# Two transformer layers on one core: 250 pairs of row maxima beside the projections in place of 223, and sixteen key tiles kept in place of twelve

## The chip, the cores and the metric

The kernel runs on one core of a Trainium2 chip. The metric is the device time of one execution in microseconds, as the median of several runs. The engines are named as in the profile: PE (TensorE matmuls), PEld (its weight loads), DVE (VectorE), ACT (ScalarE), POOL (GpSimd) and SP (SyncE, which issues most of the DMAs here).

## The reference

A block of attention A and a block of two dense layers B are applied twice, A, B, A, B, each on the normalised rows and added back to them. There are 2048 rows of 640 columns, 32 heads of 20 columns, and an inner width of 1536; both passes use the same weights.

```python
def _A_ref(x, wqkv, wo):
    qkv = (x @ wqkv).reshape(B, S, 3, H, Dh)      # transposed to 3, B, H, S, Dh
    q, k, v = qkv
    scores = einsum("bhqd,bhkd->bhqk", q, k) * (Dh ** -0.5)
    o = einsum("bhqk,bhkd->bhqd", softmax(scores), v)
    return o.transpose(0, 2, 1, 3).reshape(B, S, D) @ wo
def _B_ref(x, w1, b1, w2, b2):
    r = max(x @ w1 + b1, 0)
    return (r * r) @ w2 + b2

x = A_x
x = x + _A_ref(_layernorm(x), A_wqkv, A_wo)
x = x + _B_ref(_layernorm(x), B_w1, B_b1, B_w2, B_b2)
x = x + _A_ref(_layernorm(x), A_wqkv, A_wo)
x = x + _B_ref(_layernorm(x), B_w1, B_b1, B_w2, B_b2)
```

## The kernel before, in words

Each layer has three stages: `qkv` (the projections to queries, keys and values), `attention`, and the output projection with the dense layers (`add_heads`, `mlp`). The program is written out in a fixed order; each engine works through its instructions in that order, and waits where a semaphore says so. Matrix operands are split in a high and a low part (`split_to` on ACT and DVE, `split_on_pool` on ACT and POOL), so that a projection is three matmuls per block of 128 inner columns (`THREE`).

**Projections.** The rows are cut in four blocks `tb` of 512. `front` loads, normalises (DVE: statistics L252, L253, normalising L260) and transposes (PE, L362) one block into five tiles `xnT`. A unit (`proj_unit`, 15 matmuls, L304) makes 128 columns of queries or keys for one block; there are 40 units. `UNITS` has first the four units of each block that hold the first head groups (`FIRST` = 4), block after block, and then the other six for all four blocks. The result goes to memory (`d_qk`) through SP one unit later (`later`, `pending`). Sixteen value units (`v_unit`, 30 matmuls of 320 columns, L332) follow.

**Row maxima.** The softmax needs the maximum of each query row over all 2048 keys. A *pair* is one 128-query piece `sub` of a block of 512 queries, against one tile of 512 keys `c`, for the two heads `par` of a pair `p`: two matmuls (L433) and the maxima over their results on DVE. Heads come in groups `g` of four; a block of queries is `t = 4 g + qb`, and has 32 pairs; a layer has 32 blocks and 1024 pairs. A *group of work* `(g, qb, c)` has eight pairs.

Part of the pairs is done beside the projections: `between` is called after every projection matmul with a cost (1 for a projection matmul, 0.65 for a value matmul), and each time the sum reaches a threshold it calls `some`, which takes three pairs from the list `work`, refilled group by group from `groups`. There a pair writes two adjacent banks (`Twos`, three such pairs of banks) and one reduction reads both (`smax_two`, L454). `tiles` asks for a group's key tile and query tile (`load_k`, `load_q`: six DMAs on SP each, and two more for the rows of ones in a key tile that is made for the first time) when the group ahead of it is taken. `groups` is filled from `EARLY[tb]` at the end of the fourth unit of block `tb`, with the groups whose query and key blocks are there by then, and at the last block with all groups of head group 1.

The other pairs are done in `attention`, where each half of a pair has its own reduction (`smax`, L445).

**Attention.** Blocks follow each other; each has 16 key tiles of 128 keys. For a key tile there are four scores (L499: 62 rows of contraction, since two rows hold the maximum that is to be subtracted), four exponentials on ACT (L506) and the product with the values (L511, accumulated in bank 7). The scores of heads `par` 0 and 1 lie in different rows of the PE array, as do the two halves of a pair of maxima. The order is a string of letters: `a`, `b` a score of either half, `m`, `n` half a pair of maxima, `V` the product with the values. `ORDERS[n]` has eight key tiles (32 scores, eight `V`) and `n` pairs; `pairs` picks `n` between 12 and 16 for each round, so that no block of queries is reached by the scores before its maxima are done:

```python
most = max([8 * (e + 1 - n) / max(t * NKT - 5 - i, 1) for t, e in ends.items() if e >= n], default=0)
state["debt"] += most
n = min(max(round(state["debt"]), 12), 16)
state["debt"] -= n
```

After a block's last maximum `mrows_max` and `mrows` turn its maxima into the two extra rows of the query tile (one transposition on PE, L474, a copy on ACT, two operations on POOL, eight DMAs). After a block's last key tile `finish` copies the accumulators (ACT, L524) and POOL and SP do the division later on. `begin` does what is due when a key tile is begun: it loads queries, values, and in the first four key-tile groups of a head group the key tiles of the next head groups into `kept`, a ring of tiles indexed by `g % 3` and `c`.

All tiles of 4 KB per partition come from one pool of 42 slots.

Of the kernel before, what the change touches and what calls it, by code (L numbers as in the profile page):

```python
# [9 lines left out]
F32R = mybir.dt.float32r  # L10
# [6 lines left out]
P = 128  # L17
# [7 lines left out]
QB = 512  # L25
NQB = S // QB
NG = H // 4
# [11 lines left out]
def tile_layers(  # L39
# [26 lines left out]
    def slot(shape, dtype, label):  # L66
        return arena.tile(shape, dtype, tag="slot", name=name(label))
# [315 lines left out]
    k_t, q_t, v_t, mx_t, kept = {}, {}, {}, {}, {}  # L383
# [12 lines left out]
    def load_k(g, c, keep):  # L396

        if not keep:
            k = slot([P, 2, QB], F32R, "k")
        elif (g % 3, c) in kept:  # L400
            k = kept[g % 3, c]
        else:
            k = kept[g % 3, c] = slot([P, 2, QB], F32R, "k")
            for par in range(2):
                dma(nc.sync, k[64 * par + 60 : 64 * par + 62], d_one)
        k_t[g, c] = k
        rows_of_heads(k, 1, KSEG, g, c)
# [171 lines left out]
    def prep_job():  # L579
# [13 lines left out]
    EARLY = [  # L593
        [(0, qb, c) for qb in range(NQB) for c in range(NQB) if max(qb, c) == tb]
        for tb in range(NQB)
    ]
    EARLY[-1] += [(1, qb, c) for qb in range(NQB) for c in range(NQB)]

    FIRST = 4
# [3 lines left out]
    def qkv(first, x_src, rest):  # L605
# [4 lines left out]
        state = {"pace": 0, "n": 0}  # L610
# [13 lines left out]
            else:  # L624
                at(early, n, lambda pos=pos: w_qk.need(pos * 10, pos * 10 + 9))
        for k in range(KD if first else w_v.n):
            n = len(UNITS) - 7 + k
            if first:
                at(early, n - 2, lambda k=k: raws.append(raw_rows(wqkv[:, 2 * D :], k)))
                at(late, n, lambda k=k: w_v.put(  # L630
                    raws.pop(0), k * 4, k * 4 + 2, 2, nc.scalar.copy, pool_lo
                ))
            else:
                at(early, n, lambda k=k: w_v.load(k))
# [18 lines left out]
        def end_group(x):  # L653
            g, qb, c = x
            t = g * NQB + qb
            left[t] -= 1
            if left[t]:
                return
            if t < 1:
                mrows_max(t)  # L660
                work.append(lambda: mrows(ps_q, t))
            elif t > 2:
                del q_t[t]
# [20 lines left out]

        def between(cost):
            state["pace"] += cost
            if state["pace"] >= 11:
                state["pace"] -= 11
                some()
            state["n"] += 1  # L690
            if state["n"] % 4 == 0:
                next(rest, None)

        for n, (tb, pos) in enumerate(UNITS):
            while tb not in xt_:
                next(rest)
            run(early, n)
            later(proj_unit(pos, tb, lambda: between(1)))
            run(late, n)
            if pos == FIRST - 2:  # L700
                tiles(EARLY[tb][0])
            if pos == FIRST - 1:
                groups.extend(EARLY[tb])
            if first:
                w_qk.save_full(1)
                w_v.save_full(1)
            if pos >= FIRST and tb == NQB - 1 or n == 4 * FIRST - 1:
                w_qk.past(pos * 10 + 9, w_qk.got)
# [26 lines left out]
    def attention(first, x_src, first_rows):  # L735
# [25 lines left out]
        def begin(i):  # L761
# [6 lines left out]
                    load_q(t + 2)  # L768
            if u % 4 == 1 and qb == 0:
                k_t.pop((g - 1, u // 4), None)  # L770
                for h in (1, 2):
                    if g + h < NG and (g + h, u // 4) not in k_t:
                        load_k(g + h, u // 4, True)
                if g and g + 2 >= NG:
                    del kept[(g - 1) % 3, u // 4]
            if u in (2, 10) and qb == NQB - 1 and g + 1 < NG:
                load_v(g + 1, u // 8)
            if first and t < 16 and u % 6 == 3:
# [300 lines left out]
```

## Time and profile before

| | us |
|---|---|
| median of 3 runs | 3805.24 (3803.75 to 3805.78) |
| profiled run: time | 3801.84 |
| profiled run: span | 3799.8 |
| first layer: projections from the start to the first score | 334.2 |
| first layer: first score to the last product with the values | about 1153 |
| second layer: first score | 2224.3 |
| busy in the span: PE, DVE, ACT, POOL | 3754.3, 2923.8, 2399.9, 813.0 |
| granted clock of PE, mean | 0.997 |

The rows of the prediction come from one profiled execution. A row of a group of instructions reads: line, engine, operation, output<-input, shapes, count, then total busy microseconds and mean nanoseconds of one, then idle time of the engine just before them and who ended it. A row of the timeline reads: start, length in microseconds, engine, line, operation, count of instructions merged in it, and in brackets the idle time ahead of it and its releaser. A row of the chain of waits reads: start, length, what the end of the program was waiting for.

### The profile page before, as it was taken

The numbers are of one execution on the slowest core, as the hardware profiler recorded it, in microseconds if no ns is written. First come the engines' busy times: TensorE is split into PE (matmuls) and PEld (weight loads), VectorE is DVE, ScalarE is ACT, GpSimd is POOL, SyncE is SP. The second block draws the span as 40 slices with busy tenths as digits, with TensorE's granted clock in tenths as the row PEclk, the third lists the DMA queues.
The fourth block names the chain that finished last, engine by engine and source line by source line (L and its number), as shares of the span: only waits on it lengthen the run. The fifth ranks groups of instructions, "written<-read, shape, count | busy, mean of one in ns | idle before, by whom it ended". The sixth has DMA issues, their size and how long they took to land.

```text
span 3799.8 us, 62979 instructions
## 1 busy us (share of the span) xinstructions
PE 3754.3 (99%) x23636; PEld 2142.9 (56%) x23636; DVE 2923.8 (77%) x4436; ACT 2399.9 (63%) x4663; POOL 813.0 (21%) x889
## 2 busy tenths in 40 slices
PE   7999999999999999999999999999999999999999
PEld 5676444443443435988876754444444444369998
DVE  7999999999999992444469989999999999924443
ACT  2115999999999996122211159999999999951221
POOL 5430343221121111111143201211211111101110
PEclk9999999999999999999999999999999999999999
DMA  6553454322121135611244422222222211355111
GB/s 191 176 189 110 132 142 149 107 71 73 49 70 42 31 96 176 239 42 42 93 142 157 161 89 59 65 74 53 65 81 53 59 40 42 101 191 209 42 42 42
DMA packets 228073, 378.72 MB, mean 100 GB/s; under 512 B 47740, under 2 KB 96636, under 8 KB 227768
## 3 DMA queue, kind: packets, MB, share of 16 engines
q1 hardware_dynamic: 227224, 372.98, 31.1%
q8 instruction: 187, 3.06, 0.3%
q10 hardware_dynamic: 544, 1.71, 0.2%
q14 instruction: 118, 0.97, 0.1%
HBM read 243.00 MB, written 130.52 MB: 98 GB/s over the span
## 4 chain that ended last, share of the span: by engine, by line
PE 94%; DVE 3%; DMA 1%; ACT 1%; SPq 0%; issue 0%; POOL 0%; ACTq 0%; DVEq 0%; POOLq 0%
PE banks L511 26%; PE banks L293 20%; PE banks L499 18%; PE banks L433 18%; PE banks L304 6%; PE banks L332 4%; DVE mx L445 1%; DVE mx L454 1%; SPq L75 0%; PE banks L909 0%; PE banks L474 0%; ACT e L506 0%; DMA k<-d_qk 0%; DVE bst L252 0%; DVE h L265 0%
## 5 line engine op out<-in xcount | busy, mean ns | idle before, releaser
L506 ACT ACTIVATE e<-banks 128x512 f32<-128x512 f32 x4096 | 2113.8, 619 | 159.4 <-PE banks L499 104.7
L445 DVE TENSOR_REDUCE mx<-banks 128x1 f32<-128x512 f32 x3204 | 2002.5, 685 | 209.4 <-PE banks L433 147.5
L433 PE MATMUL banks<-k,q 60*128 60x512 f32 x4096 | 1197.5, 442 | 8.7 <-DMA q<-d_qk 4.1
L499 PE MATMUL banks<-q,k 62*128 62x512 f32 x4096 | 1174.9, 430 | 4.5 <-ACT e L506 1.7
L511 PE MATMUL banks<-e,vg 128*32 128x512 f32 x8192 | 1092.8, 605 | 0.0
L433 PEld LDWEIGHTS banks<-k,q 60*128 60x128 f32 x4096 | 580.7, 184 | 626.9 <-DVE mx L445 495.3
L499 PEld LDWEIGHTS banks<-q,k 62*128 62x128 f32 x4096 | 613.6, 185 | 438.6 <-ACT e L506 399.9
L454 DVE TENSOR_REDUCE mx<-banks 128x2 f32<-128x1024 f32 x446 | 518.8, 1220 | 49.6 <-PE banks L433 37.0
L555 POOL TENSOR_TENSOR few<-few,minus_t 128x16 f32<-128x16 f32 x62 | 179.8, 2901 | 991.1 <-DMA few<-d_s 975.3
L511 PEld LDWEIGHTS banks<-e,vg 128*32 128x32 f32 x8192 | 161.5, 108 | 346.0 <-issue 322.8
L293 PE MATMUL banks<-w,h 128*128 128x320 f32 x2304 | 352.8, 312 | 2.9 <-DVE h L265 2.7
L293 PEld LDWEIGHTS banks<-w,h 128*128 128x128 f32 x2304 | 340.9, 189 | 12.5 <-DVE h L265 6.8
L293 PE MATMUL banks<-xnT,w 128*128 128x512 f32 x1440 | 330.3, 390 | 0.0
L304 PE MATMUL banks<-xnT,wqk 128*128 128x512 f32 x1200 | 311.9, 407 | 0.0
L932 ACT ACTIVATE r<-banks,b_t 128x512 f32<-128x512 f32 x96 | 66.2, 690 | 375.2 <-PE banks L293 375.2
L293 PEld LDWEIGHTS banks<-xnT,w 128*128 128x128 f32 x1440 | 269.4, 188 | 55.3
L270 ACT COPY r<-banks 128x512 f32<-128x512 f32 x92 | 53.7, 588 | 334.9 <-PE banks L304 292.5
L304 PEld LDWEIGHTS banks<-xnT,wqk 128*128 128x128 f32 x1200 | 220.8, 192 | 68.9 <-issue 23.8
L952 DVE TENSOR_TENSOR x<-banks,x 128x320 f32<-128x320 f32 x128 | 62.8, 491 | 200.9 <-PE banks L293 194.9
L566 POOL TENSOR_TENSOR o<-o 128x512 f32<-128x512 f32 x62 | 79.5, 1282 | 560.0 <-PE banks L433 177.4
L933 DVE TENSOR_TENSOR r<-r 128x512 f32<-128x512 f32 x96 | 79.4, 827 | 132.6 <-ACT r L932 132.2
L887 DVE TENSOR_TENSOR x<-banks,x 128x320 f32<-128x320 f32 x64 | 31.0, 484 | 171.0 <-PE banks L293 77.7
(63 smaller groups left out, 1704.1 us busy)
## 6 DMA issues: line engine op xcount, KB each, us to landing
q<-d_qk SPq DMA_DIRECT2D x636, 80.0 KB
d_qk<-ev SPq DMA_DIRECT2D x80, 512.0 KB
k<-d_qk SPq DMA_DIRECT2D x384, 80.0 KB
x<-d_x SPq DMA_DIRECT2D x96, 320.0 KB
d_o<-ot SPq DMA_DIRECT2D x248, 80.0 KB
ot<-d_o SPq DMA_DIRECT2D x38, 512.0 KB
d_v<-v SPq DMA_DIRECT2D x32, 512.0 KB
vg<-d_v SPq DMA_DIRECT2D x32, 512.0 KB
```

Of the source, the lines that this page charges most:

```text
L293: nc.tensor.matmul(dst, a, b, start=(n == 0), stop=(n == last))
L304: nc.tensor.matmul(dst, w_qk.piece(pos * 10 + hw * KD + k), xt_[tb][k][:, hx, :], start=(n == 0), stop=(n == 3 * KD - 1),)
L332: nc.tensor.matmul(dst[:, :HALF], xt_[tb][k][:, hx, i * P : (i + 1) * P], w_v.piece(k * 4 + hw * 2 + hf), start=(j == 0), stop=(j == 3 * K ...
L433: nc.tensor.matmul(dst, q_t[t][b : b + 60, p, sub * P : (sub + 1) * P], k_t[t // NQB, c][b : b + 60, p, :], start=True, stop=True,)
L445: nc.vector.tensor_reduce(maxima(t)[:, 2 * p + par, sub, c : c + 1], dst, axis=AX.X, op=ALU.max)
L454: nc.vector.tensor_reduce(maxima(t)[:, 2 * p : 2 * p + 2, sub, c], dst, axis=AX.X, op=ALU.max)
L499: nc.tensor.matmul(dst, k_t[t // NQB, kt // 4][b : b + 62, p, (kt % 4) * P : (kt % 4 + 1) * P], q_t[t][b : b + 62, p, :], start=True, stop ...
L506: nc.scalar.activation(es[p][:, par, :], dst, AF.Exp, scale=SCALE)
L511: nc.tensor.matmul(acc[32 * h : 32 * h + 32, :], v_t[t // NQB, kt // 8][:, kt % 8, 32 * h : 32 * h + 32], es[p][:, par, :], start=(kt == 0 ...
L555: nc.gpsimd.tensor_tensor(few, few, minus_t, op=ALU.pow)
L566: nc.gpsimd.tensor_mul(o[:, 0, :], o[:, 0, :], o[:, 1, :])
L933: nc.vector.tensor_mul(r, r, r)
```

## The change

In the projections `between` calls `some` at every 10 units of pace, not 11. The groups of a block of rows are handed over after the first unit of the next block (`n % FIRST == 0`), not after the block's own fourth unit, and the first group's tiles are asked for one unit later; one group of head group 1 is handed over after unit 5, ahead of those of block 1. The last list holds the groups of head groups 1 and 2. The value weights are prepared from two units later on, in the second layer two slots per unit. In attention the ring of key tiles has four head groups, and `begin` loads three groups ahead.

The instructions that result: 249 pairs per layer are issued beside the projections where there were 223, and the number of matmuls is the same.

```diff
-        elif (g % 3, c) in kept:
-            k = kept[g % 3, c]
+        elif (g % 4, c) in kept:
+            k = kept[g % 4, c]
         else:
-            k = kept[g % 3, c] = slot([P, 2, QB], F32R, "k")
+            k = kept[g % 4, c] = slot([P, 2, QB], F32R, "k")
...
-    EARLY[-1] += [(1, qb, c) for qb in range(NQB) for c in range(NQB)]
+    EARLY[-1] += [(g, qb, c) for g in (1, 2) for qb in range(NQB) for c in range(NQB)][1:]
...
         for k in range(KD if first else w_v.n):
-            n = len(UNITS) - 7 + k
+            n = len(UNITS) - 5 + (k if first else k // 2)
...
             if left[t]:
+                if t >= NQB and groups and groups[0][:2] != (g, qb):
+                    del q_t[t]
                 return
...
             state["pace"] += cost
-            if state["pace"] >= 11:
-                state["pace"] -= 11
+            if state["pace"] >= 10:
+                state["pace"] -= 10
                 some()
...
             run(late, n)
-            if pos == FIRST - 2:
+            if pos == FIRST - 1:
                 tiles(EARLY[tb][0])
-            if pos == FIRST - 1:
-                groups.extend(EARLY[tb])
+            if n % FIRST == 0 and 0 < n <= NQB * FIRST:
+                groups.extend(EARLY[n // FIRST - 1])
+            if n == FIRST + 1:
+                groups.append((1, 0, 0))
...
                 k_t.pop((g - 1, u // 4), None)
-                for h in (1, 2):
+                for h in (1, 2, 3):
                     if g + h < NG and (g + h, u // 4) not in k_t:
                         load_k(g + h, u // 4, True)
-                if g and g + 2 >= NG:
-                    del kept[(g - 1) % 3, u // 4]
+                if g and g + 3 >= NG:
+                    del kept[(g - 1) % 4, u // 4]
```

## The prediction, made before the changed kernel was run

> **What bounds the kernel now.** I read the busy table first, then three stretches of the first layer in one table of windows, then the chain of waits and the timeline inside each stretch.
>
> ```profile
> PE 3754.3 (99%) x23636; PEld 2142.9 (56%) x23636; DVE 2923.8 (77%) x4436; ACT 2399.9 (63%) x4663; POOL 813.0 (21%) x889
> ...
> L445 DVE TENSOR_REDUCE mx<-banks 128x1 f32<-128x512 f32 x3204 | 2002.5, 685 | 209.4 <-PE banks L433 147.5
> ...
> L454 DVE TENSOR_REDUCE mx<-banks 128x2 f32<-128x1024 f32 x446 | 518.8, 1220 | 49.6 <-PE banks L433 37.0
> ```
> ```profile
> 86.64:215.70 129.06, 128.44 (x602) 87.67 (x601) 122.57 (x107) 20.89 (x38) 66.30 (x73) 1.00 0.54 182
> 238.12:331.80 93.68, 93.68 (x597) 77.17 (x597) 90.55 (x79) 12.82 (x30) 5.67 (x14) 1.00 0.32 114
> 350.00:1382.00 1032.00, 1031.25 (x7025) 415.00 (x7022) 937.50 (x1526) 959.09 (x1888) 260.19 (x270) 1.00 0.30 85
> ```
>
> The columns after the stretch are its length and then PE, PEld, DVE, ACT and POOL busy. The first stretch is the query/key projections, the second the value projections, the third attention. PE is never idle in any of them, but DVE is busy 95%, 97% and 91%, and ACT 93% in attention. So PE sets the pace with other engines close behind, and the question for moved work is which engine it overfills where it arrives, and how much it relieves where it leaves. The clock is 1.00 throughout.
>
> A maximum has the same two matmuls in both places. What differs is DVE: two reductions of 685 ns each in attention (L445), one of 1220 ns beside the projections (L454).
>
> **Cost where the maxima arrive.** The helper `some` issues three pairs per call. The chain of waits shows the two steady rhythms:
>
> ```profile
> 86.64 2.72 PE banks L304 x11
> 89.36 0.89 PE banks L433 x6
> ...
> 238.12 2.69 PE banks L332 x17
> 240.80 0.90 PE banks L433 x5
> ```
>
> A call therefore costs 2.72+0.90 = 3.62 us beside 11 projection matmuls, or 2.69+0.91 = 3.60 us beside 17 value matmuls; its own six matmuls take 0.90 us, 0.30 per pair. The change calls after 10 units of pace: 10/11 x 2.72+0.90 = 3.37 us and, with 10/0.65 = 15.4 value matmuls, 2.44+0.90 = 3.34 us on PE. What does DVE need for the same three pairs?
>
> ```profile
> 41.19 3.49 DVE L454 TENSOR_REDUCE mx<-banks 128x2 f32<-128x1024 f32 x3 [2.05 <-PE banks L433]
> ...
> 51.06 2.35 DVE L454 TENSOR_REDUCE mx<-banks 128x2 f32<-128x1024 f32 x2
> ...
> 270.10 28.70 DVE L454 TENSOR_REDUCE mx<-banks 128x2 f32<-128x1024 f32 x24 [0.24 <-PE banks L433]
> ```
>
> Three queued reductions last 3.49 us, two 2.35: one more costs 1.14 us, although each is 1220 ns long, so they overlap by 0.08. A saturated DVE then needs 3.42 us per call. That is more than PE's 3.37 and 3.34: **the bound of the projections passes from PE to DVE**, by a little. From the 240th projection matmul on, where both kernels run steadily, there are 360 of them and 480 value matmuls (312 units of pace). Before: 32.7 calls x 3.62 + 28.4 x 3.60 = 220.6 us. After: (36+31.2) x 3.42 = 229.8 us, **+9.2 per layer**; the lower bound, PE alone, is 36 x 3.37+31.2 x 3.34 = 225.5, +4.9.
>
> The last call also moves. It had 15 value matmuls behind it and has three now, so attention's first scores, which reuse the banks of these maxima, wait longer for DVE than they did (second layer: the last row below, 0.72 us; first layer: no wait). When the last pair is issued DVE still has almost three reductions in hand, 3.4 us, of which three matmuls and the first free bank cover about 0.9, so the wait is some 2.5 us; about half of it is the DVE surplus counted above. I add 1.2 per layer and take off the 0.7 in the second.
>
> The early part gains eight pairs per layer (49 in place of 41 before the 240th matmul), 8 x 0.30 = 2.4 us of PE. Against that stand waits that the later start may shorten:
>
> ```profile
> 39.70 0.47 PE L433 MATMUL banks<-k,q 60*128 60x512 f32 x1 [2.30 <-DMA q<-d_qk]
> 62.99 0.93 PE L433 MATMUL banks<-k,q 60*128 60x512 f32 x5 [1.07 <-DMA k<-d_qk]
> 73.21 0.33 PE L362 MATMUL banks<-ident,x 128*128 128x128 f32 x1 [1.82 <-DVE x L260]
> 218.32 0.46 PE L433 MATMUL banks<-k,q 60*128 60x512 f32 x1 [0.85 <-DMA q<-d_qk]
> 219.23 0.70 PE L433 MATMUL banks<-k,q 60*128 60x512 f32 x3 [0.45 <-DMA q<-d_qk]
> 1959.28 0.47 PE L433 MATMUL banks<-k,q 60*128 60x512 f32 x1 [1.17 <-DMA k<-d_qk]
> 1960.93 0.94 PE L433 MATMUL banks<-k,q 60*128 60x512 f32 x5 [1.18 <-DMA k<-d_qk]
> 2224.34 0.73 PE L499 MATMUL banks<-q,k 62*128 62x512 f32 x4 [0.72 <-DVE mx L454]
> ```
>
> The number in brackets is PE's idle time and who ended it. The first three (5.2 us, first layer) and the two at 1960 (2.35 us, second layer) are the starts of a block of rows; the pair at 218 is the start of head group 1. The first block's tiles are now asked for one unit later on SP too, behind one more store, so that wait mostly stays; block 1 gains, since its tiles get two more calls and about five matmuls of lead. But tile (1,0,0) is requested only when it is taken:
>
> ```profile
> 59.05 0.34 SPq L75
> ...
> 59.43 3.43 DMA k<-d_qk
> ```
>
> Its 14 DMAs (k with its two rows of ones, and q) cost 14 x 0.34 = 4.8 us on SP and 3.43 to land, 8.2 us behind the store of unit 4; PE has 24 matmuls (5.9 us) and two calls (1.8), 7.7 us. So about 0.5 us of new wait, and what queues behind PE there is DVE's statistics and normalisation for later blocks. I let half of the old waits go: -2.6 and -1.2. Bounds: all of them gone, or as many microseconds added by (1,0,0). The wait at 218 goes, because k and q of group 1 are there long before: -1.3 in the first layer, since these waits came on top of the 220.6.
>
> The value weights are prepared two units later. In the first layer the last part reaches POOL behind the last unit's split:
>
> ```profile
> L270 ACT COPY r<-banks 128x512 f32<-128x512 f32 x92 | 53.7, 588 | 334.9 <-PE banks L304 292.5 <-PE banks L362 31.3 <-DVE mx L454 6.6
> ...
> L275 POOL CAST ev<-r 128x512 fp32r<-128x512 f32 x72 | 44.0, 612 | 176.3 <-ACT r L270 176.3
> ...
> L278 POOL TENSOR_TENSOR ev<-r,ev 128x512 fp32r<-128x512 f32 x72 | 92.7, 1287 | 5.8
> ...
> L278 POOL TENSOR_TENSOR wv<-raw,wv 128x640 fp32r<-128x640 f32 x2 | 3.1, 1569 | 0.0
> ```
>
> One after the other these make 0.59+0.61+1.29+1.57 = 4.1 us after unit 39; the 14th value matmul wants the part after 13 x 2.69/17 = 2.1. The 2 us are covered by DVE's queue of up to three reductions (3.4 us); without that cover they cost 2. I cost it at nothing. Loads of group g+3 in place of g+2 are the same number per group later on; in the first four key tiles of attention both are issued, 16 DMAs x 0.34 = 5.4 us per 8.5 us, ahead of need: nothing.
>
> Sum: first layer 9.2+1.2+2.4-2.6-1.3 = 8.9; second 9.2+1.2-0.7+2.4-1.2 = 10.9. **Together +19.8** (about 8 to 30).
>
> **Gain where they leave.** A round of attention is one order string, eight key tiles, with 12 to 16 pairs. By the rule in `pairs`, before has 54 rounds of 13, six of 14, four of 12 per layer (the last three with few or no maxima); after has 40 of 13, 24 of 12. 249 pairs are done early, not 250. The timeline gives each kind's length, as the distance between starts of the value matmuls (L511), one group per key tile:
>
> ```profile
> 1380.34 1.06 PE L511 MATMUL banks<-e,vg 128*32 128x512 f32 x8
> 1382.23 1.07 PE L511 MATMUL banks<-e,vg 128*32 128x512 f32 x8
> ...
> 1384.37 1.06 PE L511 MATMUL banks<-e,vg 128*32 128x512 f32 x8
> 1387.67 1.06 PE L511 MATMUL banks<-e,vg 128*32 128x512 f32 x8
> ...
> 1400.07 1.06 PE L511 MATMUL banks<-e,vg 128*32 128x512 f32 x8
> 1401.07 0.33 PE L474 MATMUL banks<-ident,nm 128*128 128x128 f32 x1
> 1401.33 0.85 PE L433 MATMUL banks<-k,q 60*128 60x512 f32 x2
> ...
> 1403.04 1.07 PE L511 MATMUL banks<-e,vg 128*32 128x512 f32 x8
> ...
> 1417.89 1.06 PE L511 MATMUL banks<-e,vg 128*32 128x512 f32 x8
> ...
> 1436.28 1.06 PE L511 MATMUL banks<-e,vg 128*32 128x512 f32 x8
> ```
>
> 1382.23 to 1400.07 is a round of 13: 17.84 us. 1400.07 to 1417.89 is the one full round of 12, and 1417.89 to 1436.28 a round of 14: 18.39. So 14 to 13 saves 0.55, six times: 3.3 per layer. The string of 12 has seven operations in every segment, and its last seven segments take 14.85 us, 2.12 each; the string of 13 has one of eleven operations that takes 3.30 (1384.37 to 1387.67). The first segment of the 12 took 2.97, but holds a transposition (0.26) that elsewhere falls in other rounds, and a pair of maxima that took 0.85. Its floor is 2.12 plus one step; a step is 0.23, a segment of six operations taking 1.89 (1380.34 to 1382.23). So a round of 12 is 14.85 + 2.35 to 2.71 = 17.20 to 17.56. The 13 behind it loses the trailing maximum of a 13 ahead of it, another 0.23 if nothing else then waits. One round changed from 13 to 12 saves 0.28 to 0.87; I take 0.65, nearer the sum of the operations. Twenty changed: 13.0. ACT must keep up:
>
> ```profile
> 1467.72 18.55 ACT L506 ACTIVATE e<-banks 128x512 f32<-128x512 f32 x36
> ...
> L524 ACT COPY o<-banks 128x512 f32<-128x512 f32 x64 | 39.6, 619 | 2.5 <-PE banks L511 2.5
> ```
>
> Saturated, it takes 0.515 per exponential, 2.06 per segment of 2.12: it fits, with 0.5 us to spare in a round, and half the rounds also hold a copy of 0.62. I take off 1.0. Gain 3.3+13.0-1.0 = 15.3 per layer, **30.6 in both** (14 to 41).
>
> **Sum.** 19.8-30.6 = -10.8. The profiled run took 3801.84, giving 3791.0; it lies 3.4 under the median of the timed runs, 3805.24, against which I forecast **3794**. 0.2% of the time, 7.6 us, is about what a measurement of this kernel can tell from no change.
>
> **Rivals.** (A) A saved pair is worth only its own step on PE, 0.235, because the ragged string of 13 and ACT give the rest back in mixed sequences. 26 x 0.235 x 2 = 12.2: +7.6, 3813. For it: one full 12 round is all there is, and it saved little as a whole. Against: seven even segments of 2.12 in a row. 0.08.
>
> (B) Slower: in a queue that never empties, reductions keep their whole 1220 ns. A call is 3.66, 0.24 more than I take, 67.2 calls and two layers: 32 us, net +21.5, 3827. It decides from 1.17 us per reduction, where -10.8 is used up. Against: the 3.49 and 2.35 above, though never over a long full queue, since PE paced all 24 in 28.70. 0.07. The Trainium skill (VectorE: DVE Perf Modes, "The DRAIN you can't avoid") says that the next operation does not start until the pipe is empty; by that rule it would be this rival, and the trace's three in 3.49 disagree.
>
> (C) The unprefetched (1,0,0), value weights or doubled k loads stall PE by some 4 us more per layer: 3802, no difference. 0.08.
>
> (D) The starts lose all their waits and DVE's surplus is soaked up, so that PE's own bound holds: 2 x 4.3 for the calls, 3.8 for the starts and some 1.6 of the wait at the end of the calls, 14 us less, 3780. 0.08.
>
> **How the numbers follow.** The forecast has 0.69, with its own range 3782 to 3806, most of it under 3797.6. Faster: 0.59 of that and D, 0.67. Same: 0.10, C and half of A, 0.22. Slower: B and half of A, 0.11. The range 3781 to 3811 leaves out B, the worse half of A and D's tail.
>
> **What would show it.** Right: calls beside projections about 3.42 apart with no idle gap on DVE; rounds of 12 at 17.2 to 17.6 and no 18.4; attention some 15 us shorter and projections some 10 longer per layer. Wrong: calls at 3.6 apart (B), rounds of 12 over 17.7 (A), or PE waiting for k at the third call (C).

## The result, and the profile after

The changed kernel takes 3835.4 us (median of four executions, 3833.2 to 3839.7) against 3804.5 for the kernel before (3802.8 to 3805.8): a ratio of 1.0082, 95% interval 1.0067 to 1.0097. It is slower by about 31 us, where I had forecast 3794 and a range up to 3811. Its profiled run took 3839.7 with a span of 3837.7, 37.9 us more than the profiled run of before; the rows below come from it.

The first table is worked out from the starts of single instructions in the two traces: the 241st projection matmul of a layer, the first and the last value matmul, the first score, the last product with the values.

| stretch, us | layer 1 before | after | layer 2 before | after |
|---|---|---|---|---|
| first projection matmul to the 241st | 92.3 | 102.6 | 78.9 | 83.5 |
| 241st to the first value matmul | 121.7 | 127.5 | 119.8 | 127.1 |
| value matmuls | 101.7 | 110.4 | 101.7 | 109.4 |
| last value matmul to first score | 0.2 | 1.5 | 1.0 | 1.6 |
| attention | 1153.1 | 1153.7 | 1151.4 | 1142.4 |

The dense layers in between and the tail are the same within 0.1 us. So three things are to be explained: the steady stretch (rows two and three) grew by 14.5 and 15.0 us, where I had 7.9 and 9.2 (9.2 each, less 1.3 for the wait at 218 us that goes in the first layer); the start grew by 10.2 and 4.6, where I had about nothing; and attention gave 9.0 in the second layer and nothing in the first, where I had 15.3 in each.

The busy table and the two groups of maxima, on the page of the changed kernel:

```profile
PE 3779.8 (98%) x23636; PEld 2150.7 (56%) x23636; DVE 2919.5 (76%) x4384; ACT 2396.2 (62%) x4663; POOL 813.7 (21%) x889
...
L445 DVE TENSOR_REDUCE mx<-banks 128x1 f32<-128x512 f32 x3100 | 1941.7, 684 | 260.3 <-PE banks L433 175.1
...
L454 DVE TENSOR_REDUCE mx<-banks 128x2 f32<-128x1024 f32 x498 | 574.0, 1218 | 41.1 <-PE banks L433 36.1
```

The work moved as planned: 498 double reductions in place of 446 and 104 single ones fewer. PE is busy 25 us longer with the same 23636 matmuls, so part of the loss hides inside its busy time. Some of it is the clock: the granted clock is at half in 41.0 us of this run, in pieces of 3.4, against 20.5 us in the profiled run of before (1.00 in the rest). Where PE has work throughout, a piece costs 1.7 us, so the difference is worth up to 10 us, an estimate from these lengths.

**The steady stretch.** Busy time by windows of the changed kernel, the two halves of the first layer's steady stretch (length, PE, PEld, DVE, ACT, POOL busy):

```profile
120.72:248.10 127.38, 126.60 (x577) 82.40 (x575) 123.19 (x109) 20.20 (x38) 61.00 (x67) 1.00 0.52 180
248.10:358.50 110.40, 108.69 (x668) 85.21 (x665) 107.48 (x94) 13.90 (x33) 10.05 (x19) 1.00 0.34 121
```

Both engines are at 97% to 99%, and neither is full. The chain of waits in the second layer shows why:

```profile
2036.82 2.49 PE banks L304 x10
2039.31 0.90 PE banks L433 x6
2040.21 2.51 PE banks L304 x10
2042.72 1.11 PE banks L433 x4
2043.83 2.49 PE banks L304 x10
2046.32 0.92 PE banks L433 x5
```

The maxima take PE 0.90 in one call and 1.1 in the next, so calls alternate between 3.39 and 3.6 us. In the longer ones the third pair stands until DVE has freed its bank. The waits of PE's weight loads and DVE's timeline in the 40 us from 2034, some 11 calls:

```profile
PEld banks L433 <- DVE mx L454: 3.2, 11, 0.4
```
```profile
2033.92 40.82 DVE L454 TENSOR_REDUCE mx<-banks 128x2 f32<-128x1024 f32 x35
```

At 40.82/35 = 1.166 us a reduction, 3.50 a call, DVE is not full either: in a full queue they start 1.136 us apart (pace9, below). From the two halves together, 237.9 us for 67.2 calls, a call is 3.54 us in the first layer, and 236.5/67.2 = 3.52 in the second; I had 3.42.

**The start.** PE's waits in the first layer, changed kernel (timeline; idle time and its cause in brackets):

```profile
42.32 0.50 PE L433 MATMUL banks<-k,q 60*128 60x512 f32 x1 [1.80 <-DMA q<-d_qk]
43.88 1.48 PE L433 MATMUL banks<-k,q 60*128 60x512 f32 x5 [1.06 <-DMA q<-d_qk]
58.35 0.76 PE L433 MATMUL banks<-k,q 60*128 60x512 f32 x1 [3.06 <-DMA q<-d_qk]
78.29 0.50 PE L433 MATMUL banks<-k,q 60*128 60x512 f32 x2 [1.52 <-DVE mx L454]
81.77 1.11 PE L362 MATMUL banks<-ident,x 128*128 128x128 f32 x4 [2.98 <-DVE mx L454]
```

The wait at 58 is the group (1,0,0), which nobody asked for ahead. Before the one at 81.77 PE wants to transpose block 2, and DVE's normalisation of it stands behind reductions. This wait is longer than before but not new: PE's waits for DVE in the stretch to the 241st matmul come to 5.6 us, against 3.1 in the kernel before and 4.3 in tiles16 (below), which has the same start as before. DVE's timeline there:

```profile
77.02 1.22 DVE L454 TENSOR_REDUCE mx<-banks 128x2 f32<-128x1024 f32 x1
78.15 2.43 DVE L260 TENSOR_SCALAR x<-x,mv 128x640 f32<-128x640 f32 x2
80.50 3.48 DVE L454 TENSOR_REDUCE mx<-banks 128x2 f32<-128x1024 f32 x3
```

PE's waits for DMAs in the same stretch are 6.5 us against 3.8, and its clock is at half for 13.6 us against 10.2. One such piece lies at the wait at 58 (windows, columns as above; the 0.50 is the granted clock), another at the first scores of the second layer:

```profile
57.70:64.50 6.80, 5.54 (x16) 4.07 (x17) 2.23 (x4) 0.83 (x2) 2.01 (x3) 0.50 0.25 95
2272.90:2279.70 6.80, 6.76 (x26) 3.26 (x24) 3.20 (x6) 5.26 (x11) 0.00 (x0) 0.50 0.58 150
```

So a wait of PE costs more than its own length here. In the first layer the waits (+5.2), the clock (about +1.7) and the eight pairs more (+2.4 by the price of the prediction) make 9.3 of the 10.2 us. In the second layer PE's waits are the same as before, 3.4 us; the eight pairs account for half of its 4.6, and the rest stays open.

**Attention.** The waits of ACT in the first 400 us of the first layer's attention; the second row had no counterpart in the trace of before:

```profile
ACT e L506 <- PE banks L499: 13.3, 43, 1.4
ACT e L506 <- POOL ot L278: 10.2, 5, 2.8
```

An exponential waits for POOL to finish `ot`, a tile of `divide` with which it has no data in common. What they share is the pool of 42 slots.

And the lengths of rounds (a 12 or a 13 is a round with 12 or 13 pairs; "behind" names the round ahead of it), as starts of the value matmuls at the ends of five rounds in the second layer (PE timeline, changed kernel):

```profile
2382.01 0.64 PE L511 MATMUL banks<-e,vg 128*32 128x512 f32 x4
2400.11 0.64 PE L511 MATMUL banks<-e,vg 128*32 128x512 f32 x4
2417.69 0.64 PE L511 MATMUL banks<-e,vg 128*32 128x512 f32 x4
2435.74 0.64 PE L511 MATMUL banks<-e,vg 128*32 128x512 f32 x4
2453.56 0.64 PE L511 MATMUL banks<-e,vg 128*32 128x512 f32 x4
```

In order: a 13 behind a 13 with a transposition, 18.10; a 12 behind it without one, 17.58; a 13 behind that 12 with one, 18.05; a 13 behind a 13 without, 17.82. Over all rounds of this layer without a transposition the means are 17.84 (13 behind 13), 17.60 (12 behind 13) and 17.70 (13 behind 12): a 12 among 13s is worth 0.24 itself and some 0.14 in the round behind it, 0.4 us and not 0.65. Twenty of them, and six 14s that became 13s at 0.6, make 11.6 us; behind the first round the second layer's attention is 11.3 us shorter. The first round gives 2.3 back: its scores wait for DVE, and the granted clock is at half for 6.8 us (the row at 2272.90), where in the kernel before it stayed at 1.00.

### The profile page after: what moved, and what is told of

It reads as the page before. It is cut to its first block, busy times and chain, and to the rows that moved or that the text cites. A ratio compares the mean times of both kernels' runs of the same rounds, so it can differ in the third digit from the quotient of the medians.

```text
span 3837.7 us, 62954 instructions
## 1 busy us (share of the span) xinstructions
PE 3779.8 (98%) x23636; PEld 2150.7 (56%) x23636; DVE 2919.5 (76%) x4384; ACT 2396.2 (62%) x4663; POOL 813.7 (21%) x889
## 3 DMA queue, kind: packets, MB, share of 16 engines
q8 instruction: 187, 3.06, 0.3%
## 4 chain that ended last, share of the span: by engine, by line
PE 91%; DVE 4%; DMA 2%; POOL 1%; ACT 1%; SPq 1%; issue 1%; ACTq 0%; POOLq 0%; DVEq 0%
PE banks L511 26%; PE banks L293 19%; PE banks L499 19%; PE banks L433 16%; PE banks L304 6%; PE banks L332 3%; DVE mx L454 2%; SPq L75 1%; DMA d_qk<-ev 0%; PE banks L913 0%; PE banks L474 0%; DVE bst L252 0%; PE banks L362 0%; DVE x L260 0%; DVE h L265 0%
## 5 line engine op out<-in xcount | busy, mean ns | idle before, releaser
L445 DVE TENSOR_REDUCE mx<-banks 128x1 f32<-128x512 f32 x3100 | 1941.7, 684 | 260.3 <-PE banks L433 175.1
L433 PE MATMUL banks<-k,q 60*128 60x512 f32 x4096 | 1198.2, 445 | 11.6 <-DMA q<-d_qk 8.3
L499 PE MATMUL banks<-q,k 62*128 62x512 f32 x4096 | 1158.8, 432 | 10.9 <-ACT e L506 5.6
L433 PEld LDWEIGHTS banks<-k,q 60*128 60x128 f32 x4096 | 567.8, 185 | 537.4 <-DVE mx L445 378.6
L454 DVE TENSOR_REDUCE mx<-banks 128x2 f32<-128x1024 f32 x498 | 574.0, 1218 | 41.1 <-PE banks L433 36.1
L956 DVE TENSOR_TENSOR x<-banks,x 128x320 f32<-128x320 f32 x128 | 62.8, 490 | 200.6 <-PE banks L293 191.4
L332 PE MATMUL banks<-wv,xnT 128*128 128x320 f32 x960 | 158.2, 316 | 1.7 <-POOL wv L278 1.3
```

The source lines that it names most:

```text
L332: nc.tensor.matmul(dst[:, :HALF], xt_[tb][k][:, hx, i * P : (i + 1) * P], w_v.piece(k * 4 + hw * 2 + hf), start=(j == 0), stop=(j == 3 * K ...
L433: nc.tensor.matmul(dst, q_t[t][b : b + 60, p, sub * P : (sub + 1) * P], k_t[t // NQB, c][b : b + 60, p, :], start=True, stop=True,)
L445: nc.vector.tensor_reduce(maxima(t)[:, 2 * p + par, sub, c : c + 1], dst, axis=AX.X, op=ALU.max)
L454: nc.vector.tensor_reduce(maxima(t)[:, 2 * p : 2 * p + 2, sub, c], dst, axis=AX.X, op=ALU.max)
L499: nc.tensor.matmul(dst, k_t[t // NQB, kt // 4][b : b + 62, p, (kt % 4) * P : (kt % 4 + 1) * P], q_t[t][b : b + 62, p, :], start=True, stop ...
```

## The experiments

All times are medians beside runs of the kernel before on the same chip, which took 3807.1 to 3807.6 in the four sets. The columns behind the ratio are read like the first table, first layer / second layer; the kernel before has 92.3 / 78.9, 223.4 / 221.5 and 1153.1 / 1151.4, the changed one 102.6 / 83.5, 237.9 / 236.5 and 1153.7 / 1142.4. These columns come from one profiled execution each. The letters of theories and rivals are those of the expectations; each says what it stands for.

| run | us | ratio to before, 95% | start | steady | attention |
|---|---|---|---|---|---|
| pace10 | 3823.3 | 1.0041 [1.0026, 1.0056] | 95.7 / 76.1 | 241.7 / 236.1 | 1145.3 / 1143.9 |
| tiles16 | 3816.6 | 1.0024 [1.0015, 1.0034] | 95.2 / 76.6 | 223.9 / 221.4 | 1163.0 / 1151.3 |
| start | 3810.9 | 1.0008 [0.9999, 1.0018] | 98.7 / 80.0 | 225.2 / 221.5 | 1152.3 / 1153.4 |
| after12 | 3826.5 | 1.0049 [1.0032, 1.0066] | 102.4 / 82.8 | 237.5 / 236.4 | 1142.3 / 1142.3 |
| pace9 | 3832.2 | 1.0063 [1.0040, 1.0085] | 105.0 / 85.0 | 256.2 / 254.8 | 1127.8 / 1120.6 |
| three_quarters | 3804.2 | 0.9988 [0.9977, 0.9999] | 96.8 / 82.0 | 229.0 / 226.5 | 1142.4 / 1141.5 |
| one_pair | 3937.0 | 1.0336 [1.0306, 1.0366] | 103.4 / 96.2 | 283.3 / 282.3 | 1142.9 / 1142.3 |
| ask_ahead | 3824.5 | 1.0045 [1.0029, 1.0061] | 97.2 / 82.3 | 238.2 / 236.6 | 1143.5 / 1142.2 |
| runs12 | 3812.8 | 1.0014 [1.0005, 1.0023] | 100.5 / 85.5 | 238.1 / 236.7 | 1134.0 / 1134.6 |
| pace105 | 3820.2 | 1.0038 [1.0024, 1.0052] | 98.5 / 81.4 | 234.1 / 230.1 | 1147.0 / 1148.4 |
| pace105g | 3818.3 | 1.0030 [1.0019, 1.0041] | 99.2 / 79.4 | 234.2 / 230.0 | 1145.1 / 1147.1 |
| pace9g | 3832.6 | 1.0068 [1.0055, 1.0080] | 103.1 / 83.2 | 260.3 / 254.8 | 1123.0 / 1123.9 |
| prep_later | 3833.3 | 1.0067 [1.0049, 1.0085] | 100.9 / 81.7 | 237.8 / 236.6 | 1145.8 / 1142.0 |
| pace10g | 3807.9 | 0.9999 [0.9990, 1.0009] | 95.3 / 77.1 | 239.7 / 236.0 | 1136.5 / 1137.6 |
| value16 | 3806.5 | 0.9998 [0.9989, 1.0007] | 94.6 / 79.0 | 228.2 / 225.6 | 1147.6 / 1148.8 |

The column of the start is the loosest: up to there before and tiles16 have the same instructions, and differ by 2.8 and 2.3 us. The steady stretch repeats within about 1 us in the second layer.

### The change taken apart

**pace10**: the kernel before, with

```diff
-            if state["pace"] >= 11:
-                state["pace"] -= 11
+            if state["pace"] >= 10:
+                state["pace"] -= 10
```

> The kernel before with one edit, the threshold of the pace 10 in place of 11 (about 245 pairs per layer beside the projections; 45 rounds of 13 and 19 of 12 in attention). The sum of the prediction: calls 3.42 us apart, +9 to +10 us per layer in the projections, 0.65 x 15 + 0.55 x 6 = 13 us less in attention: about 7 us faster than before, 3797. Theory T (a call is 3.50, because a third pair waits for its bank and a pair after a wait takes 0.43 us of PE and not 0.235; a round changed from 13 to 12 saves 0.40): +14 to +16 per layer in the projections, -9 in attention, no 10 us of stalls of ACT behind POOL in the first layer: about 12 us slower, 3816. If the stalls of ACT behind POOL do come, they are from the pace and not from the sixteen tiles: 3826.

16 us slower than before: theory T's mechanism and not the sum, though 4 us more than T had. The steady stretch grew by 18.3 and 14.6, attention shrank by 7.8 and 7.5, and ACT does not wait for `ot`. The first layer has some 4 us that the second has not: this kernel keeps the wait for the tiles of head group 1 (1.4 us at 217.7), and the granted clock is at half from 218.4 to 225.2. **tiles16**: the kernel before, with the ring `kept` at `g % 4` and `for h in (1, 2, 3)`.

> The kernel before with one edit, sixteen kept key tiles in place of twelve, loads three groups ahead; the pairs and the rounds of attention stay as before. The prediction costed this at nothing: no difference. Theory T: the four tiles more take slots of the pool in the first layer, where the preparation of the later weights takes some too, so the exponentials wait for POOL's o: about 10 us in the first layer's attention, the second layer's as before: 3815. If it makes no difference, the stalls of the changed kernel need the shorter rounds or the other start as well.

9.5 us slower, and the trace puts 9.9 of it in the first layer's attention and nothing elsewhere that lies outside the scatter of the start. **start**: the kernel before with the other `EARLY`, the hand-over at `n % FIRST == 0` and the group (1,0,0) after unit 5.

> The kernel before with only the other start: groups handed over one unit later, one group of head group 1 taken ahead of block 1 and not asked for ahead, the last list with two head groups; threshold of the pace 11, twelve tiles. The prediction's terms: waits of 2.6 and 1.2 us fewer, 1.3 fewer in the first layer, a few pairs more beside the projections: between -5 and 0 us. Theory T: the unprepared group stalls PE for its tiles, and the normalisation of block 1 queues behind its reductions on DVE: +10 us in the first layer, +4 in the second by the 240th projection matmul, attention 1 to 2 us shorter per layer: 3815. If it is less, part of the early loss belongs to the shorter pace.

About 4 us, less than theory T had, and just at the edge of what can be told. The three parts sum to 16.2+9.5+3.8 = 29.5, against 31 for the whole. By stretches the sum holds less well: in the first layer's steady stretch the parts make 20.6 and the whole 14.5, since the other start does away with the wait at 217.7, while attention of the second layer gives 5.6 in the parts and 9.0 in the whole. **after12**: the changed kernel with `g % 3` and `for h in (1, 2)` again.

> The changed kernel with the ring of twelve tiles back (loads two groups ahead); everything else as changed (40 rounds of 13, 24 of 12). Theory T: the 10 to 11 us of stalls of ACT behind POOL in the first layer's attention go, the second layer stays: 3825, 10 us faster than the changed kernel. Rival (the stalls come from the shorter rounds, which leave POOL behind): they stay, 3835. Rival (a key tile is loaded too late with two groups ahead): PE waits for k in attention, over 3835.

The first layer's attention fell by 11.4 us to that of the second, and ACT's waits for `ot` are gone. Rows of ACT's waits of this kernel, same stretch of attention:

```profile
ACT e L506 <- PE banks L499: 13.1, 42, 1.4
ACT e L506 <- PE banks L433: 8.4, 28, 1.5
```

### Why a call takes 3.5 us

From here on the changed kernel with twelve tiles (after12) is the base. **pace9**: threshold 9 in place of 10.

> The changed kernel with twelve tiles and the threshold of the pace at 9: more calls (74.7 in place of 67.2 from the 240th projection matmul of a layer to its last value matmul, a stretch of 237.5 us with threshold 10), so 48 rounds of 12 in attention. Theory L (a call is 3.50 to 3.53 us at threshold 10 because PE and DVE wait for each other in turn: the third pair waits for DVE to free its bank, and with 10 units behind it the next call's first pair is then late for DVE by about 0.2): with 9 units PE is 0.25 us earlier, DVE has no gap, a call is 3.42 us and the stretch 255 us. Rival D (3.52 is DVE's own rate in a long queue): 263. Rival P (nothing but PE's own work, 2.22+0.90 us): 233. Attention about 8 us shorter per layer than with threshold 10, at 0.37 us a pair.

Theory L held: 256.2 and 254.8 us, 3.42 a call, and now one engine does bound. Its chain of waits in the second layer, one row for 15 calls:

```profile
2079.73 51.14 DVE mx L454 x45
```

51.14/45 = 1.136 us a reduction, with no gap. Attention was shorter by 14.5 and 21.7 than with threshold 10, not by 8: a miss that led to runs12 below. (The first layer has one round of 23.7 us in it, in which ACT waits 3.3 for `ot` even with twelve tiles.) **three_quarters**: `dst` became `dst[:, :, :384]` in the reduction of `smax_two`.

> The changed kernel with twelve tiles, where each reduction beside the projections reads 384 of the 512 results of each half: the maxima are then over three quarters of the keys of such a tile, so the work of PE is the same and that of DVE smaller, at about 0.95 us a reduction. Theory L: with DVE out of the way a call costs PE's 2.47+0.90 = 3.37 us, and the stretch from the 240th projection matmul to the last value matmul is 225 to 228 us in place of 237.5. Rival S (the 3.5 us are PE's own, because projections cost more between maxima): it stays at 237. The early part loses the 3 us of wait for DVE at the second block's transpositions too.

229.0 and 226.5 us, one just above and one in the expected range, near PE's own 67.2 x 3.37 = 226.5, with even calls. The first layer's start fell by 5.6, where some 3 were expected. Rows of its chain of waits and of DVE's timeline, second layer:

```profile
2112.53 2.49 PE banks L304 x10
2115.03 0.89 PE banks L433 x5
2115.91 2.49 PE banks L304 x10
2118.41 0.90 PE banks L433 x6
```
```profile
2115.49 2.69 DVE L454 TENSOR_REDUCE mx<-banks 128x2 f32<-128x768 f32 x3 [0.70 <-PE banks L433]
```

So PE's price of a call and DVE's were both right. What failed is the rule that the longer of the two is the length. Between 3.37 and 3.42 the engines take turns in waiting: the third pair of a call needs the bank that DVE frees last, and the first pair of the next call has to reach DVE before it runs dry; a wait of the one is not made up by the other. **pace105**, the kernel before with threshold 10.5, shows it largest.

> The kernel before with one edit, the threshold of the pace 10.5 in place of 11: 64 calls in place of 61.1 in the steady stretch, 57 rounds of 13 and 7 of 12, mixed. PE's own need is 2.59+0.90 = 3.49 us a call, above DVE's 3.42. By the sum of the prediction PE sets the pace and the stretch is 223 to 224 us, 2 to 3 more than PE's 220.6; theory L (the two engines still wait for each other when calls fall after 10 and 11 matmuls in turn): 3.53 to 3.55 us a call, 226 to 227. Attention 9 pairs fewer at 0.37, 3.3 us less per layer. By the sum: 3806; by L: 3811.

Beside the units calls come after 10 and 11 matmuls in turn. Chain of waits and DVE's timeline, second layer:

```profile
2097.99 1.13 PE banks L433 x6
2099.12 2.76 PE banks L304 x11
2101.88 0.90 PE banks L433 x6
2102.78 2.53 PE banks L304 x10
2105.31 1.09 PE banks L433 x5
```
```profile
2102.36 6.92 DVE L454 TENSOR_REDUCE mx<-banks 128x2 f32<-128x1024 f32 x6 [0.40 <-PE banks L433]
2109.59 4.62 DVE L454 TENSOR_REDUCE mx<-banks 128x2 f32<-128x1024 f32 x4 [0.31 <-PE banks L433]
```

A call of 10 finds its third bank still taken and waits 0.2 (1.1 in place of 0.90); the call of 11 behind it has more work of its own, 3.62, than DVE's 3.42, so that delay stays, and DVE then idles 0.3 to 0.4. Two calls take 7.24 us, 3.62 on average: as long as with 11 throughout, though an average call needs only 3.49. The run was worse than both expectations, 3820. **one_pair** spreads the same pairs evenly: `some(1)` at each 10/3 units of pace.

> The changed kernel with twelve tiles, where the same pairs are called one at a time, at each 10/3 units of pace, in place of three at each 10. Rival B (three pairs in a row run out of banks; evenly spread, they never wait): the stretch from the 240th projection matmul to the last value matmul is DVE's 3.42 a three, 230 us in place of 237.5. Theory L has a second cost in it, what PE pays each time it goes from projections to a pair and back: a pair after a wait took 0.43 us against 0.235 behind another pair. Then three single pairs cost 1.29 in place of 0.90, a three 3.76 us, and the stretch is 250 to 253.

283 us, far beyond either. Rows of its PE timeline, second layer:

```profile
2154.29 1.21 PE L304 MATMUL banks<-xnT,wqk 128*128 128x512 f32 x4
2155.44 0.49 PE L433 MATMUL banks<-k,q 60*128 60x512 f32 x2
2155.86 0.98 PE L304 MATMUL banks<-xnT,wqk 128*128 128x512 f32 x3
2156.77 0.50 PE L433 MATMUL banks<-k,q 60*128 60x512 f32 x2
2157.20 0.98 PE L304 MATMUL banks<-xnT,wqk 128*128 128x512 f32 x3
```

From start to start a single pair takes 0.43, as I had it, but three projection matmuls between pairs take 0.91 in place of 3 x 0.247 = 0.74: PE pays on the way back too. That was in neither theory, and no run here says why.

### The start

**ask_ahead**: after12, with the tiles of (1,0,0) asked for when the groups of block 0 are handed over:

```diff
                 groups.extend(EARLY[n // FIRST - 1])
+                if n == FIRST:
+                    tiles((1, 0, 0))
```

> The changed kernel with twelve tiles, where the tiles of the group of head group 1 that is taken ahead of block 1 are asked for one unit before that group is handed over. If the early loss (10 us to the 240th projection matmul in the first layer, 4 in the second) is the wait for those tiles and what it delays on DVE: 3 to 4 us less there, with the wait of 3 us at about 58 us gone. If SP's queue as such is late (the loads stand behind waits for stores): the wait moves and stays about 3 us, and the stretch is as long as before. The rest as with twelve tiles, 3826: 3822 or 3826.

The wait of 3 us at 58 is gone and the first layer's start shorter by 5.2; the second's by 0.5. The median fell by 2, within the scatter. So about half of the first layer's loss is the late request, as far as one trace with a scatter of 2 to 3 us can tell. The wait of 3 us for DVE at the transpositions stayed, so it does not follow from the one at 58; with threshold 10 alone (pace10) there is one of 2.7.

### Rounds of 12

**runs12**: after12, with the pairs of a round rounded up from the rate, which sorts the same 40 rounds of 13 and 24 of 12:

```diff
-            n = min(max(round(state["debt"]), 12), 16)
-            state["debt"] -= n
+            n = min(max(int(-(-most // 1)), 12), 16)
```

> The changed kernel with twelve tiles, where the number of pairs of a round of attention is the rate that the next dates ask for, rounded up, in place of the running debt: the same 40 rounds of 13 and 24 of 12, but all the 13 first and then all the 12. In the trace with the threshold at 9 a round of 12 behind a 12 took 17.0 us without a transposition, behind a 13 it took 17.59; a 13 behind a 12 17.67, behind a 13 17.84. Theory M (the mixed sequence is what gives the gain back: each stretch of 12 in between costs 17.59+17.67-17.84-17.00 = 0.42 us): 21 such places go, 8.8 us less attention per layer, 3809. Rival (12s are short only because of what the threshold 9 did elsewhere, or ACT bounds a long run of them): rounds of 12 stay at 17.6, 3826.

Attention fell by 8.3 and 7.7 us, nearly the 8.8 expected, and the time by 13.7. Rounds of 12 behind a 12, starts of the value matmuls as above, second layer:

```profile
3063.15 0.64 PE L511 MATMUL banks<-e,vg 128*32 128x512 f32 x4
3080.15 0.64 PE L511 MATMUL banks<-e,vg 128*32 128x512 f32 x4
3097.57 0.64 PE L511 MATMUL banks<-e,vg 128*32 128x512 f32 x4
3114.58 0.64 PE L511 MATMUL banks<-e,vg 128*32 128x512 f32 x4
```

17.00, 17.42 (with a transposition), 17.01. In a run of its kind a 12 is 0.84 shorter than a 13; alone among 13s half of that is lost. The intervals inside the rounds say where: the first segment of a 12 takes 2.70 us behind a 13, whose last letter is a maximum that still has to be done, and 2.11 behind a 12; the other seven are the same.

**pace105g** is pace105 with that rounding, **pace9g** the kernel before with threshold 9, two head groups in the last list, and that rounding.

> The same with threshold 10.5 and the number of pairs of a round rounded up from the rate, so the rounds of 13 come first and the 7 of 12 last. Theory M: 2 to 3 us per layer less than with them mixed, some 5 us below the run with threshold 10.5 alone: 3802 to 3806.

3818, above the range, because pace105 itself was; the difference between the two is 2 us where 5 were expected, and 1.3 to 1.9 us per layer in attention.

> The kernel before with its own start and twelve tiles, threshold 9 with two head groups in the last list, and the number of pairs of a round rounded up from the rate: 29 rounds of 13, then 35 of 12. DVE sets the pace beside the projections at 3.42 us a call, 255 us for the steady stretch against 222: +33 per layer, the early part 0 to 3. Theory M: 13s at 17.84 and 12s at 17.0 (0.26 and 0.41 more with a transposition) against 54 of 13, six of 14 and four of 12 before: attention 34 to 37 us less per layer. Sum -4 to +2 per layer: 3800 to 3811, about the time of before, though each part moved by over 30 us. If the mixed rounds are not the cause, attention is only 25 to 30 us shorter: 3815 to 3825.

3833, a miss. The steady stretch came as expected (+37 and +33). The start was 11 and 4 longer, not 0 to 3, and attention 30 and 28 shorter, not 34 to 37. For the latter my sum was at fault and not the theory: by the lengths given there, 25 rounds fewer of 13, six fewer of 14 and 31 more of 12 make 29 us.

### What was still open

**prep_later**: the changed kernel, sixteen tiles, with `first and 8 <= t < 24` in place of `first and t < 16` where `begin` calls `prep_job`.

> The changed kernel with its sixteen tiles, where the preparation of the weights of the output projection and the dense layers runs beside blocks 8 to 23 of the first layer's attention in place of 0 to 15. Theory S (the slots of the pool are used up by sixteen tiles and the pieces of weights in preparation together): the stalls of ACT behind POOL, 10 us in rounds 4 to 20, leave those rounds and come again some 16 rounds later, about the same in sum: 3835. Rival (they come from the start of attention, its loads and the first blocks): they stay in rounds 4 to 20. Rival (any time would do but the first 16 rounds, which also hold the loads of three head groups): they go altogether, 3825.

The stalls left rounds 4 to 20 and some came back in rounds 23 to 28, but only 3.5 us of them (1145.8 against 1142.3 with twelve tiles). So the preparation is the other half of the cause, and its place sets the size. No run had a pool with more slots: that it is the slots which run out is inferred from the waits for `ot`, which go with four tiles fewer and move with the preparation.

**pace10g** is pace10 with the rounding, **value16** the kernel before with `between(0.6875)` for value matmuls and the rounding.

> The kernel before with threshold 10 and the number of pairs of a round rounded up from the rate: 45 rounds of 13, then 19 of 12. By theory M the attention is 15 to 17 us shorter per layer than before, and by theory L the steady stretch 14 to 18 longer, the early part 0 to 3: the two even out, 3804 to 3812, against 3823 with the rounds mixed.

> The kernel before with a value matmul counted at 0.6875 in place of 0.65, so that a call comes after 16 value matmuls, always, in place of 17 (threshold 11, calls beside the units unchanged), and the number of pairs of a round rounded up: 60 rounds of 13, 4 of 12, none of 14. 30 calls in the value stretch in place of 28.2. By PE alone a call is 2.54+0.90 = 3.44 us and the stretch 103; with waits as in theory L 3.50 to 3.55, 105 to 107 against 101.7. Attention 6 x 0.55 = 3.3 us less per layer and perhaps 1 more. Sum between -3 and +1 per layer: 3800 to 3809.

Both are the same as before within 0.1%. In value16 all calls come after 16 value matmuls, and PE needs 3.44 us, above DVE's 3.42; still they alternate between 3.43 and 3.62, 3.53 on average. No version that computes the whole beat the kernel before; three_quarters, 0.1% under it, leaves a quarter of the keys out of the early maxima.

## Why the prediction was wrong

The forecast was 10.8 us less and the profiled run took 37.9 more. Of these 48.7 us the steady stretch makes 12.4, the start 13.8, the sixteen tiles 11.4 and the rest of attention 10.8: four steps failed, by nearly the same amount.

**The length of a call**: the step "the bound of the projections passes from PE to DVE", with 3.42 us as the larger of two needs. The needs were right (3.37 in three_quarters, 3.42 in pace9). With two engines that hand three pairs of banks to each other and are within 0.1 us, the length was 3.54 and 3.52, above both: 67.2 x 0.12 and 67.2 x 0.10 are the 8.1 and 6.7 us by which the stretches exceed my 229.8. The kernel before also took more than my 220.6 (223.4 and 221.5; 1.3 of the 223.4 is the wait at 218, which I had apart), so the difference missed by 6.6 and 5.8.

**The start**: "I let half of the old waits go" and "about 0.5 us of new wait". Measured over the four kernels with the changed start, threshold and order of the first 240 matmuls (after, after12, runs12, prep_later) it is 101.6 and 83.4 on average, against 94.0 and 78.2 for the three with the first part as before (before, tiles16, value16): +7.6 and +5.2 where I had -0.2 and +1.2. I counted 14 issues of 0.34 us, 4.8 in all, and the landing, but not that SP stands still between issues until earlier DMAs have landed. SP's timeline and waits in the changed kernel, first layer, while it issues the loads of (1,0,0):

```profile
47.13 0.65 SPq L75 DMA_DIRECT2D k<-d_one  x2
48.01 5.88 SPq L75 DMA_DIRECT2D k<-d_qk  x6
53.93 2.56 SPq L75 DMA_DIRECT2D q<-d_qk  x6
```
```profile
SPq L75 <- DMA x<-in_A_x_dram: 3.1, 4, 1.4
SPq L75 <- DMA d_qk<-ev: 1.1, 1, 1.1
```

The 14 issues took 9.4 us (47.13 to 56.49), and by the profile 3.1 of that was for the landing of four loads of rows, which a key tile does not read. That part of rival C was right: PE waited 3.06 us for (1,0,0). I also named DVE's statistics as queued behind that wait and gave them no price; PE's waits for DVE did grow, from 3.1 to 5.6 us, but the longest of them stayed in ask_ahead, where the wait for (1,0,0) is gone. And I read the clock only where it is 1.00 and put no price on what follows a wait.

**Sixteen tiles** were costed "at nothing" from SP's side. They cost 9.5 us alone and 11.4 in the changed kernel, by all signs through slots of the pool, which the prediction never looked at. The Trainium skill (Perfetto Trace Analysis, "Optimization Strategy") says that the same gap repeating on an engine can mean too little memory for the next tile. The trace agrees in kind, though these gaps were five, 10.2 us in all, and on ACT in one layer only.

**A saved pair in attention.** The counts of rounds were right, but no 12 had the forecast length of 17.2 to 17.56 without a transposition: behind a 13 it took 17.60, behind its own kind 17.0. In the sequence that the rule of the debt makes, nearly every 12 stands alone between 13s and saves 0.4, not 0.65. Behind the first round attention is 11.3 to 11.7 us shorter (after in the second layer, after12 in both), not 15.3, and the first round takes 0.9 to 2.3 longer. This is rival A's mechanism ("the ragged string of 13 and ACT give the rest back in mixed sequences"), at some 0.44 us for each of 26 pairs and not its 0.235. The runs give ACT no part in it: in runs12 long runs of 12s keep their 17.0. I had the row for it: the first segment of the only full 12 took 2.97, and I reasoned that away.

**Right**: the 249 pairs (not the title's 250), the wait at the end of the calls (+1.3 and +0.5 against +1.2 and +0.5, the clock behind it left out), and the wait at 218 us, which is gone. The value weights, costed at nothing, brought one wait of 1.3 us in the first layer; the text had named 2 as the price without cover. Rival B named the right sign and, by luck, nearly the time, 3827, by a wrong mechanism: reductions in a full queue start 1.136 us apart over 45 of them. The Trainium skill (VectorE: DVE Perf Modes, "The DRAIN you can't avoid") has the next operation wait for an empty pipe unless it is one "that is not held", which "starts earlier"; by the 1.136 against 1.21 us of one, these are not held.

## What to carry to other kernels

When a change brings two engines that share a few buffers to within some per cent of each other, do not take the longer need as the length of a step. Here, with needs within 2% of each other, a step took 2.6% to 3.7% more than the longer one (3.52 to 3.54 for 3.42, 3.53 for 3.44, 3.62 for 3.49); with one engine some 9% ahead or more (pace9, three_quarters) it took the longer need. Price it from a run of such a step, and keep one engine clearly ahead. What a unit of moved work saves depends on its neighbours: take it from the same sequence of rounds that the planner will produce, not from the best round or a sum of operations. Look at the granted clock just behind each wait as well as in the steady stretches. Before more tiles are kept, count the slots at the fullest moment; a pool that runs out shows as a wait for an engine with which the waiter shares no data.

## What was not expected of the hardware

Going from a full-height matmul to a pair of maxima and back costs PE on both ways: 0.43 us for a lone pair against 0.30 in a group of three, and three projection matmuls in 0.91 us against 0.74 in a row. Queued reductions of 1024 values started 1.136 us apart. Those of 768 values lasted 0.95 each and three in a row 2.69, so they started 0.87 apart; a line through the two makes 1.04 ns a value and 0.07 us for all else, an estimate. And at several waits of PE of 1 to 3 us the granted clock fell to half for 3.4 or 6.8 us (from 44.0, 57.7 and 81.6 us in the changed kernel), while the waits of 0.85 and 0.45 at 218 in the kernel before left it at 1.00. Four projection matmuls from 61.18 took 2.05 us in the changed kernel, against 1.17 from 52.25 in ask_ahead, where the clock is 1.00.
